# A dynamic convolution and two matmuls on one core: the tile of products in two parts, the softmax one superblock earlier, a slice of the products on VectorE, and other loads of x

## The chip, the cores and the metric

The kernel runs on one core of one Trainium2 chip. The metric is the device time of one execution in microseconds (us), the median over runs. Each core has TensorE (PE, with its weight loads shown apart as PEld), VectorE (DVE), ScalarE (ACT), GpSimd (POOL) and SyncE (SP), which here only issues transfers. The core's 16 DMA engines carry the transfers that SP issues (the profile calls that queue hardware_dynamic, q1) and those that POOL issues (software_dynamic, q0).

## The reference

The input x has 8 batches of 4096 tokens of 192 channels. For every token, each of 8 heads (24 channels each) has 7 weights; a softmax over the 7 weights mixes the token and the six tokens before it. The result goes through two matrices with an activation between them:

```python
w = exp(weight_gen - max);  w = w / sum(w)             # over the 7 taps
x_pad = concatenate([zeros(6 tokens), x])              # per batch: a batch starts with six tokens of zeros
y[s, h, g] = sum over k of w[s, h, k] * x_pad[s + k, h, g]
h = y @ w_in                                           # 192 -> 2048
out = (h - tanh(h)) @ w_out                            # 2048 -> 192
```

## The kernel before

**Tiling.** The 32,768 tokens are cut into NTOT = 32 superblocks of 1024 tokens, four to a batch (NSB = 4). Partition p of the 128 holds tokens 8p to 8p+7 of the superblock (J = 8), and six tokens of halo ahead of them, so a tile of x (`x_t`) is 128 rows of 14 x 192 float32, 10,752 bytes a row.

**The steps of one superblock n.**
- `load_wg` and `load_x` fetch the raw weights and x, through SP. In `load_x` the transfer `rows(0, P)` brings all 128 rows; at the first superblock of a batch (s == 0) a second one, `no_halo`, then writes zeros over the halo of row 0. It writes what the first wrote, so SP waits for the first to land. Superblock 0 has its own code: 112 rows and 15 rows for the halo.
- `softmax_exp` (ACT), `softmax_sum` in two halves (DVE), and `softmax_norm` (DVE: reciprocals into a spare corner of a PSUM tile, then `scale`) make the weights `wsm`.
- `products` (POOL) multiplies x with the seven taps into `pr`, a bfloat16 tile of 7 x 8 x 192 per partition, in a pool of two. In one instruction a tap has 1536 elements per partition. From superblock 5 on the order on POOL is: taps 0 and 1; the second sum of the superblock before (below); taps 2 to 5; `dma_sum`; tap 6.
- `dma_sum` is a transfer from POOL's queue that adds one part of `pr` to another inside SBUF: taps 3 to 5 onto 0 to 2. It leaves four parts (6, 0, 1, 2). For superblocks in `TWO_SUMS` (from 13 on, those whose number is no multiple of three), `second_sum` later adds tap parts 2 and 6 onto 0 and 1, and two parts are left. The second sum is issued from inside the next superblock's `products`, and POOL waits there until the first has landed. For superblocks 2 to 4 (`PART`) one sum leaves five parts.
- `conv_sums` (PE) adds the remaining parts and transposes them into PSUM (`pc`) by matmuls with an identity; with four parts there are 96 such matmuls in a superblock, with two 48. `conv_out` (ACT) copies them to `convT`.
- `gemm1` (PE) makes one of 16 blocks of the hidden layer in PSUM (`ph`, a pool of three that `pc` shares); ACT takes its tanh, DVE subtracts (`gt`).
- `out_stream` is the second matmul, as a stream of steps (16 to each of 8 token blocks) that `out_pairs` draws from; `store_out` copies a block out (ACT) and, once per superblock, SP stores it.

**The order.** The program is written in the order of the main loop, and each engine and SP's queue keeps that order. Pass n of the loop runs, for f = 0 to 15, `gemm1(n, f)` and the steps that `STEADY` puts behind that f: `pairs[f]` steps of the second matmul, which belong to superblock n-1; the transposes of superblock n+1 at f = 13 and 14 (`t2`, `t1`); the softmax of n+3 (exp at f = 1, sums at f = 2 and 5, scale at f = 14); and at f = 1 `products(n + 2)`. `load_x(n + 3)` stands at f = 7 (`X_AT`) and is tied behind that pass's last subtraction; `load_wg(n + 4)` at f = 1.

Of the kernel before, what the change touches and what calls it, by code (L numbers as in the profile page):

```python
# [8 lines left out]
FP32 = mybir.dt.float32  # L9
BF16 = mybir.dt.bfloat16  # L10
# [6 lines left out]
def kernel(  # L17
# [8 lines left out]
    nc = tc.nc  # L26

    B, S, D = x.shape
    H, K = weight_gen.shape[2], weight_gen.shape[3]
    G = D // H  # L30
# [10 lines left out]
    NTOT = B * NSB  # L41
    NFT = F // P
    NC = D // R
    PLAIN = (0, 1)
    PART = tuple(range(2,5))
    TWO_SUMS = tuple([n for n in range(13,NTOT) if n%3])
    SUM_FIRST = tuple(range(5,32))
    SCALE_TWICE = True
    assert S % TOK == 0 and D % R == 0 and F % P == 0
    assert NFT == 2 * J, "one token block of the second matmul per pair of f tiles"  # L50

    const = ctx.enter_context(tc.tile_pool(name="const", bufs=1))
    xpool = ctx.enter_context(tc.tile_pool(name="xpool", bufs=2))
    wgpool = ctx.enter_context(tc.tile_pool(name="wgpool", bufs=2))
    ppool = ctx.enter_context(tc.tile_pool(name="ppool", bufs=2))
    cpool = ctx.enter_context(tc.tile_pool(name="cpool", bufs=2))
    tpool = ctx.enter_context(tc.tile_pool(name="tpool", bufs=3))
    gpool = ctx.enter_context(tc.tile_pool(name="gpool", bufs=2))
# [25 lines left out]
    last_exp = {}  # L84
    last_conv = {}
    first_halo = {}

    def order(inst, other, reason):
        tc.add_manual_dep(
# [16 lines left out]
    def load_x(n, behind=None):  # L106
        b, s = divmod(n, NSB)
        s0 = s * TOK

        x_t = xpool.tile([P, HALO + J, D], FP32, name="x_t")  # L110

        def rows(p0, p1, r0=0, r1=HALO + J):
            first = x[0, 0:1]
            return nc.sync.dma_start(
                out=x_t[p0:p1, r0:r1, :],
                in_=bass.AP(
                    tensor=first.tensor,
                    offset=first.offset + (b * S + s0 + p0 * J - HALO + r0) * D,
                    ap=[[J * D, p1 - p0], [D, r1 - r0], [1, D]],
                ),  # L120
            )

        def no_halo():
            nc.sync.dma_start(
                out=x_t[0:1, 0:HALO, :],
                in_=zero[:].rearrange("o (h d) -> o h d", h=1).to_broadcast([1, HALO, D]),
            )


        if n == 0:  # L130
            rows(0, P, HALO, HALO + J)
            rows(16, P, 0, HALO)
            rows(1, 16, 0, HALO)
            no_halo()
        else:
            dma = rows(0, P)
            if behind is not None:
                order(dma, behind, "order of the loads")
            if s == 0:

                no_halo()
        x_of[n] = x_t

    def softmax_exp(n):
        wg_t = wg_of.pop(n)
        e_t = wgpool.tile([P, J, H, K], FP32, name="e_t")
        last_exp[0] = nc.scalar.activation(  # L147
            out=e_t[:].rearrange("p j h k -> p (j h k)"),
            in_=wg_t[:].rearrange("p j h k -> p (j h k)"),
            func=ACT.Exp,  # L150
        )
        e_of[n] = e_t

    def softmax_tile():
        return wgpool.tile([P, J, H, K], FP32, name="wsm")

    def softmax_sum(n, j0=0, j1=J):

# [10 lines left out]
            zr_of[n] = wgpool.tile([P, J * H], FP32, name="zr")  # L169
        nc.vector.reciprocal(zr_of[n][:, j0 * H : j1 * H], zsum_of[n][:, j0 * H : j1 * H])  # L170

    def softmax_norm(n, bank):

        wsm = softmax_tile()
        zr_v = bank[:, 512 - J * H : 512]
        nc.vector.reciprocal(zr_v, zsum_of[n][:])  # L176

        def finish():
            scale(nc.vector, wsm[:], e_of[n], zr_v)
            wsm_of[n] = (wsm, None, None, None)  # L180

        return finish

    def softmax_norm_ramp(n, bank):
# [25 lines left out]
            zr.rearrange("p (n o) -> p n o", o=1).to_broadcast([P, J * H, K]),  # L210
        )

    def dma_sum(pr, k0, k1, src0, src1, step=1):
        nc.gpsimd.dma_start(  # L214
            out=pr[:, k0:k1].rearrange("p k j d -> p k (j d)"),
            in_=pr[:, src0:src1:step].rearrange("p k j d -> p k (j d)"),
            accum_op=mybir.AluOpType.add,
            max_dma_last_dim=2 * J * D,
        )

    def products(n, taps=None, sums=None, hooks={}):

        x_t = x_of.pop(n)
        wsm, wsm_v, e_t, zr = wsm_of.pop(n)
        if e_t is not None:
            scale(nc.gpsimd, wsm[:], e_t, zr[:])

        pr = ppool.tile([P, K, J, D], BF16, name="pr")
        x_v = x_t[:]
        step = x_v.ap[0]  # L230

        def mul(eng, k0, k1, j0=0, j1=J):

            w = wsm_v if eng is nc.vector else wsm[:]
            nj = j1 - j0
            return eng.tensor_mul(  # L236
                pr[:, k0:k1, j0:j1, :].rearrange("p k j (h g) -> p k (j h) g", h=H),
                bass.AP(
                    tensor=x_v.tensor,
                    offset=x_v.offset + (k0 + j0) * D,  # L240
                    ap=[step, [D, k1 - k0], [G, nj * H], [1, G]],
                ),
                w[:, j0:j1]
                .rearrange("p j h (k o) -> p k (j h) o", o=1)[:, k0:k1]
                .to_broadcast([P, k1 - k0, nj * H, G]),
            )

        def parts(*ks):
            return [[pr[:, k] for k in ks]] * NC

        if taps is not None:
            for eng, k0, k1, j0, j1 in taps:
                m = mul(eng, k0, k1, j0, j1)
                if j1 == 1:
                    first_halo[0] = m
                if k0 in hooks:
                    hooks[k0]()
            prods_of[n] = parts(*sums)
            return

        if n in PLAIN:
            mul(nc.gpsimd, 0, 3)
            mul(nc.gpsimd, 3, 5)
            mul(nc.gpsimd, 5, K)
            prods_of[n] = parts(*range(K))
        elif n in PART:
            mul(nc.gpsimd, 0, 2)
            mul(nc.gpsimd, 2, 4)
            dma_sum(pr, 0, 2, 2, 4)
            mul(nc.gpsimd, 4, K)  # L270
            prods_of[n] = parts(4, 5, 6, 0, 1)
        else:
            mul(nc.gpsimd, 0, 2)
            second_sum(n - 1)
            mul(nc.gpsimd, 2, 6)
            if n in SUM_FIRST:
                dma_sum(pr, 0, 3, 3, 6)
            mul(nc.gpsimd, 6, K)
            if n not in SUM_FIRST:
                dma_sum(pr, 0, 3, 3, 6)  # L280
            if n in TWO_SUMS:
                to_sum[n] = pr
                prods_of[n] = parts(0, 1)
            else:
                prods_of[n] = parts(6, 0, 1, 2)
            if n == NTOT - 1:
                second_sum(n)

    def second_sum(n):

        if n in to_sum:
            dma_sum(to_sum.pop(n), 0, 2, 2, K, 4)

    def conv_sums(n, parts, pcs, home=None):

# [53 lines left out]
    def gemm1(n, f):  # L349
# [17 lines left out]
        last_act[0] = nc.scalar.activation(out=th[:], in_=ph_f, func=ACT.Tanh)  # L367
        last_sub[0] = nc.vector.tensor_sub(gt[:], ph_f, th[:])  # L368
        g_of.setdefault(n, []).append(gt)

    LAST = (NTOT - 1) * J
    half = {}
# [139 lines left out]
    for c in range(NC):  # L512
# [2 lines left out]
    nc.sync.dma_start(out=w_in[R:P, :, FA:F], in_=w_in[0:R, :, FA:F])  # L515
    products(
        1,
        taps=[(V, 0, 1, 0, J), (V, 1, 2, 0, J), (G_, 2, 5, 0, J), (G_, 5, 7, 0, J)],
        sums=range(K),
        hooks={2: load_w_out},  # L520
    )
    conv(0, (0, 1), (2,))
    softmax_exp(2)
    load_x(2)
    softmax_norm_ramp(2, obank[0])
    products(2)

    def some(sums, m):
        for _ in range(m):
# [24 lines left out]

    STEADY = dict(pairs=(4, 12, 0, 16, 0, 16, 0, 16, 0, 6, 10, 6, 10, 8, 8, 16), t1=(14, 8), t2=(13, 0), scale=14, sums=(2, 5))
    FIRST = dict(pairs=(4, 12, 0, 16, 1, 15, 0, 16, 0, 16, 0, 13, 3, 0, 16, 16), t1=(15, 2), t2=(11, 10), scale=15, sums=(1, 2, 3, 4, 8, 10))
    X_AT = 7

    def transposes(n, chunks):
        pcs = []
# [2 lines left out]
        conv_out(n, (chunks,), pcs)  # L565
        return pcs[0]

    for n in range(1, NTOT):
        more = n < NTOT - 1
        finish = None  # L570
        plan = FIRST if n == 1 else STEADY
        for f in range(NFT):
            gemm1(n, f)
            if n == 1:
                if f == 1:
                    load_wg(5)
# [5 lines left out]
                        step(m, h * JH, (h + 1) * JH)  # L582
                if f == 5:
                    wsm_of[3] = (softmax_tile(), None, e_of[3], zr_of[3])
                    products(3)
            elif f == 1:
                if n + 3 < NTOT:
                    softmax_exp(n + 3)
                if n + 4 < NTOT:
                    load_wg(n + 4)  # L590
                if n < NTOT - 2:
                    products(n + 2)
            if n > 1 and n + 3 < NTOT:
                for h, at in enumerate(plan["sums"]):
                    if f == at:
                        softmax_sum(n + 3, h * JH, (h + 1) * JH)
            if f == X_AT and n + 3 < NTOT:
                load_x(n + 3, last_sub[0])
            done = 0
            for chunks, at in sorted((((0, 1), plan["t2"]), ((2,), plan["t1"])), key=lambda c: c[1]):  # L600
                if more and at[0] == f:
                    out_pairs(at[1] - done)
                    done = at[1]
                    pc = transposes(n + 1, chunks)
                    if chunks == (2,) and n + 3 < NTOT:
                        finish = softmax_norm(n + 3, pc[:, 0])
            if finish is not None and f >= plan["scale"]:
                finish()
                finish = None
            out_pairs(plan["pairs"][f] - done)  # L610

    gemm2_last(0, 0, J)
# [34 lines left out]
```

The softmax here doesn't subtract the row's maximum and nothing guards it: scores larger than these inputs give would overflow.

## Time and profile before

| | |
|---|---|
| median of 3 runs | 754.72 us (754.22 to 755.33) |
| the profiled execution | 753.12 us, of it 751.4 us span |
| PE busy | 725.4 us, 97% |
| DVE busy | 664.6 us, 88% |
| POOL busy | 668.9 us, 89% |
| ACT busy | 638.8 us, 85% |
| DMA engines: POOL's queue, SP's queue | 35.7% and 27.6% of 16 engines' span |

Shares are of the span. A PE that is busy is not thereby at its peak, since its matmuls overlap. A row of the groups gives the line, engine and operation, what it writes and reads, its shape and how often it ran, then the time it was busy, the mean of one, and the idle time just before it with what ended that. A line of the waits gives who waited for whom: us in total, how often, the longest. In a timeline the first number is the start, the second the duration, "x3" three instructions merged. A line of the windows gives for a stretch of the span its length, then the busy time of each engine.

### The profile page before, as it was taken

Reading aid. Unit: us, or ns where it says so; the run is one execution under the profiler, and the core shown is the slowest. Engines: PE = TensorE matmul, PEld = TensorE weight load, DVE = VectorE, ACT = ScalarE, POOL = GpSimd, SP = SyncE. Lnnn points to the kernel's source line nnn. Section 1 sums busy time; section 2 is a strip of 40 time slices with the busy share of each in tenths; the row PEclk is TensorE's granted clock in tenths of the full one; section 3 lists DMA queues with packets and bytes.
Section 4 is the critical chain, followed back from the end, with each engine's and each line's share of the span. In section 5 each row is a group of like instructions: output and inputs, shape, how many; then the busy total and the mean of one; then the engine's idle time right before and its main releaser. Section 6 shows DMA issues by size and latency. Waiting matters only on the chain.

```text
span 751.4 us, 30497 instructions
## 1 busy us (share of the span) xinstructions
PE 725.4 (97%) x13928; PEld 567.6 (76%) x13928; DVE 664.6 (88%) x655; ACT 638.8 (85%) x872; POOL 668.9 (89%) x150
## 2 busy tenths in 40 slices
PE   3899999999999999999999999999999699999998
PEld 2477887787887777777777777777787577777777
DVE  7999889998889998999999999999989589998983
ACT  4888888888888888898989899898989588988883
POOL 7999999999999999999999999999999988999000
PEclk9999999999999999999999999999999899999999
DMA  8944526665655567785796777579668658673412
GB/s 234 242 111 107 171 109 173 187 181 126 191 149 170 169 170 160 202 196 163 196 229 151 180 203 185 169 196 215 173 157 192 180 139 189 183 177 85 113 44 86
DMA packets 32511, 124.99 MB, mean 166 GB/s; under 512 B 4495, under 2 KB 9343, under 8 KB 28414
## 3 DMA queue, kind: packets, MB, share of 16 engines
q0 software_dynamic: 17664, 46.01, 35.7%
q1 hardware_dynamic: 14718, 77.03, 27.6%
q8 instruction: 109, 1.79, 0.9%
q14 instruction: 20, 0.16, 0.1%
HBM read 54.52 MB, written 25.17 MB: 106 GB/s over the span
## 4 chain that ended last, share of the span: by engine, by line
PE 49%; DMA 4%; POOL 4%; issue 0%; ACT 0%; DVE 0%; POOLq 0%; DVEq 0%
PE obank L389 23%; PE ph L354 22%; DMA pr<-pr 4%; POOL pr L236 4%; PE pc L311 2%; PE po L432 1%; ACT th L367 0%; DVE wsm L207 0%; POOL pr L214 0%; ACT convT L337 0%; DVE pc L176 0%; DVE out_sb L446 0%; ACT ot L445 0%; DVE gt L368 0%; POOLq L214 0%
## 5 line engine op out<-in xcount | busy, mean ns | idle before, releaser
L368 DVE TENSOR_TENSOR gt<-ph,th 128x1024 bf16<-128x1024 f32 x512 | 603.1, 1218 | 66.8 <-ACT th L367 66.2
L236 POOL TENSOR_TENSOR pr<-x_t,wsm 128x3072 bf16<-128x3072 f32 (+3 forms) x95 | 629.7, 6816 | 8.1 <-PE obank L389 3.4
L367 ACT ACTIVATE th<-ph 128x1024 f32<-128x1024 f32 x512 | 506.8, 1026 | 71.1 <-PE ph L354 66.9
L354 PE MATMUL ph<-convT,w_in 64*128 64x512 bf16 x3072 | 407.3, 380 | 5.0 <-DVE gt L368 3.2
L389 PEld LDWEIGHTS <-gt 64*128 64x128 bf16 x7936 | 353.0, 94 | 73.0 <-issue 11.7
L389 PE MATMUL obank<-w_out,gt 64*128 64x192 bf16 x7936 | 399.5, 243 | 0.6 <-issue 0.5
L354 PEld LDWEIGHTS <-w_in 64*128 64x128 bf16 x3072 | 171.5, 95 | 82.7 <-issue 12.2
L408 ACT ACTIVATE out_sb<-obank 128x192 f32<-128x192 f32 x248 | 82.4, 332 | 12.9 <-PE obank L389 10.4
L214 POOL DMA_DIRECT2D pr<-pr x43 | 54.9, 1276 | 20.4 <-DMA pr<-pr 11.0
L311 PEld LDWEIGHTS <-pr 64*128 64x128 bf16 x2664 | 51.9, 102 | 24.1 <-POOL pr L236 10.2
L311 PE MATMUL pc<-ident,pr 64*128 64x64 bf16 x2496 | 50.7, 194 | 16.6 <-POOL pr L236 10.1
L337 ACT ACTIVATE convT<-pc 128x1024 bf16<-128x1024 f32 (+1 forms) x62 | 50.5, 816 | 7.3 <-PE pc L311 6.7
L161 DVE TENSOR_REDUCE zsum<-e_t 128x32 f32<-128x224 f32 (+1 forms) x61 | 23.6, 387 | 3.0 <-ACT e_t L147 3.0
L147 ACT ACTIVATE e_t<-wg_t 128x448 f32<-128x448 f32 x32 | 18.2, 569 | 7.3 <-DMA wg_t<-in_weight_gen_dram 7.3
L207 DVE TENSOR_TENSOR wsm<-e_t,pc 128x448 f32<-128x448 f32 x28 | 17.4, 621 | 3.3 <-POOL pr L236 0.5
L176 DVE RECIPROCAL pc<-zsum 128x64 f32<-128x64 f32 x28 | 15.4, 551 | 0.1
L432 PE MATMUL po<-w_out,gt 64*128 64x192 bf16 x256 | 11.2, 243 | 0.0
L236 DVE TENSOR_TENSOR pr<-x_t,obank 128x1536 bf16<-128x1536 f32 (+4 forms) x8 | 10.3, 1349 | 0.6 <-ACT wsm L199 0.6
L432 PEld LDWEIGHTS <-gt 64*128 64x128 bf16 x256 | 10.8, 93 | 0.0
L446 DVE TENSOR_TENSOR out_sb<-po,ot 128x192 f32<-128x192 f32 x8 | 2.9, 358 | 9.0 <-ACT ot L445 9.0
L445 ACT ACTIVATE ot<-po 128x192 f32<-128x192 f32 x8 | 2.6, 331 | 7.3 <-PE po L432 7.3
L467 POOL DMA_DIRECT2D w_in<-in_moe_w_in_dram x4 | 2.5, 628 | 3.0 <-ACT e_t L147 3.0
(19 smaller groups left out, 18.3 us busy)
## 6 DMA issues: line engine op xcount, KB each, us to landing
x_t<-in_x_dram SPq DMA_DIRECT2D x31, 1344.0 KB, 6.0
pr<-pr POOLq DMA_DIRECT2D x27, 1152.0 KB, 9.9
out_dram<-out_sb SPq DMA_DIRECT2D x31, 768.0 KB, 3.4
pr<-pr POOLq DMA_DIRECT2D x16, 768.0 KB, 6.8
wg_t<-in_weight_gen_dram SPq DMA_DIRECT2D x32, 224.0 KB, 6.8
x_t<-in_x_dram SPq DMA_DIRECT2D x1, 768.0 KB
w_out<-in_moe_w_out_dram POOLq DMA_DIRECT2D x1, 768.0 KB, 9.6
out_dram<-out_sb SPq DMA_DIRECT2D x4, 192.0 KB, 3.9
```

The costliest lines, as they stand in the source:

```text
L147: last_exp[0] = nc.scalar.activation(out=e_t[:].rearrange("p j h k -> p (j h k)"), in_=wg_t[:].rearrange("p j h k -> p (j h k)"), func=ACT ...
L161: nc.vector.reduce_sum(out=zsum_of[n][:, j0 * H : j1 * H], in_=e_of[n][:, j0:j1].rearrange("p j h k -> p (j h) k"), axis=AX.X,)
L214: nc.gpsimd.dma_start(out=pr[:, k0:k1].rearrange("p k j d -> p k (j d)"), in_=pr[:, src0:src1:step].rearrange("p k j d -> p k (j d)"), acc ...
L236: return eng.tensor_mul(pr[:, k0:k1, j0:j1, :].rearrange("p k j (h g) -> p k (j h) g", h=H), bass.AP(tensor=x_v.tensor, offset=x_v.offset ...
L311: nc.tensor.matmul(pc[r][:, col : col + R] if home else pc[:, r, col : col + R], lhsT=prods[c][gi][r * R : (r + 1) * R, 2 * j : 2 * j + 2] ...
L337: last_conv[0] = nc.scalar.activation(out=out, in_=pc[:, :, 0:cols].rearrange("p r (cj t) -> p r cj t", t=R), func=ACT.Copy,)
L354: nc.tensor.matmul(ph[:, r, :], lhsT=w_in[r * R : (r + 1) * R, c, f * P : (f + 1) * P], rhs=convT[r * R : (r + 1) * R, c, :], start=(c == ...
L367: last_act[0] = nc.scalar.activation(out=th[:], in_=ph_f, func=ACT.Tanh)
L368: last_sub[0] = nc.vector.tensor_sub(gt[:], ph_f, th[:])
L389: mm = nc.tensor.matmul(po[:, 0:D], lhsT=g_of[n][f][r * R : (r + 1) * R, col : col + P], rhs=w_out[r * R : (r + 1) * R, f, :], start=(r == ...
L408: last_act[0] = nc.scalar.activation(out=out_sb[:, j, :], in_=po[:, 0:D], func=ACT.Copy)
L432: nc.tensor.matmul(po[:, r, 0:D], lhsT=g_of[n][f][r * R : (r + 1) * R, col : col + P], rhs=w_out[r * R : (r + 1) * R, f, :], start=(f == 0 ...
```

## The change

1. `pr` becomes two tiles: `pa` with taps 0 to 3 (three buffers) and `pb` with taps 4 to 6 (one buffer). For superblock 1, taps 4 to 6 lie in two tiles borrowed from the pool of the output tiles.
2. POOL's order per superblock becomes: taps 0 and 1; taps 2 and 3; the second sum of the superblock before; taps 4 to 6; the first sum (`pa` 0 to 2 += `pb`).
3. From superblock 4 on (`HELP`), VectorE makes the last of the eight token columns of taps 0 and 1, 384 of the 10,752 elements. It stands at f = 3 of the pass and first copies the 16 weights into the `ph` tile that f = 3 has just left; POOL's first instruction leaves this column out.
4. `TWO_SUMS` holds every superblock from 13 to 31, also 15, 18, 21, 24, 27 and 30.
5. The softmax runs for n+4 instead of n+3. Pass 4 does two, and pass 5 does its own late. The exponential is written over the raw weights (`wg_t`, three buffers), and `wsm` has a pool of four. Its sums stand at f = 1 and 13.
6. `load_x(n + 3)` stands at f = 1 and is tied behind POOL's first instruction in `products(n + 2)`. At the first superblock of a batch (4, 8, ..., 28) the zeros go first, then one transfer brings row 0 without its halo, and one brings rows 1 to 127.
7. `pairs` is laid out differently; its sum is the same 128.

```diff
-    TWO_SUMS = tuple([n for n in range(13,NTOT) if n%3])
+    KA, KH = 4, 2
+    TWO_SUMS = (13, 14, ..., 31)
+    AHEAD = 4
+    HELP = (4, 5, ..., 31)
+    HELP_AT = 3
-    wgpool = ctx.enter_context(tc.tile_pool(name="wgpool", bufs=2))
-    ppool = ctx.enter_context(tc.tile_pool(name="ppool", bufs=2))
+    wgpool = ctx.enter_context(tc.tile_pool(name="wgpool", bufs=3))
+    papool = ctx.enter_context(tc.tile_pool(name="papool", bufs=3))
+    pbpool = ctx.enter_context(tc.tile_pool(name="pbpool", bufs=1))
+    wspool = ctx.enter_context(tc.tile_pool(name="wspool", bufs=4))
...
         else:
-            dma = rows(0, P)
+            if s == 0:
+                no_halo()
+                rows(0, 1, HALO)
+            dma = rows(1 if s == 0 else 0, P)
             if behind is not None:
                 order(dma, behind, "order of the loads")
-            if s == 0:
-                no_halo()
...
+        x_after[n + 1] = mul(nc.gpsimd, 0, KH, 0, J - 1 if n in HELP else J)
+        mul(nc.gpsimd, KH, KA)
+        second_sum(n - 1)
+        def rest(ph=None):
+            if n in HELP:
+                w = ph[:, 0, 0 : KH * H].rearrange("p (k h) -> p k h", k=KH)
+                nc.vector.tensor_copy(w, wsm[:, J - 1].rearrange("p h k -> p k h")[:, 0:KH])
+                nc.vector.tensor_mul(
+                    pa[:, 0:KH, J - 1, :].rearrange("p k (h g) -> p k h g", h=H), ...)
+            if n in PART:
+                dma_sum(pa[:, 0:2], pa[:, 2:4])
+            mul(nc.gpsimd, KA, K)
+            if n in PART:
+                prods_of[n] = parts(4, 5, 6, 0, 1)
             else:
-                prods_of[n] = parts(6, 0, 1, 2)
+                dma_sum(pa[:, 0:3], pb[:, 0:3])
+                if n in TWO_SUMS:
+                    to_sum[n] = pa
+                    prods_of[n] = parts(0, 1)
+                else:
+                    prods_of[n] = parts(3, 0, 1, 2)
+                if n == NTOT - 1:
+                    second_sum(n)
+        return rest
...
-    STEADY = dict(pairs=(4, 12, 0, 16, 0, 16, 0, 16, 0, 6, 10, 6, 10, 8, 8, 16), ..., sums=(2, 5))
+    STEADY = dict(pairs=(5, 11, 0, 16, 4, 12, 6, 10, 0, 6, 10, 8, 8, 8, 8, 16), ..., sums=(1, 13))
...
+        soft = [m for m in (n + 3,) * (n <= AHEAD) + (n + 4,) * (n >= AHEAD) if m < NTOT]
...
-            if f == X_AT and n + 3 < NTOT:
-                load_x(n + 3, last_sub[0])
+            if f == (9 if n == 1 else HELP_AT) and n + 2 < NTOT:
+                rest(ph)
+            if f == (9 if n == 1 else 1):
+                emit_x(n + 3)          # load_x(m, x_after.pop(m, None))
+                if soft and n != AHEAD and soft[0] + 1 < NTOT and n > 1:
+                    load_wg(soft[0] + 1)
```

## The prediction, made before the changed kernel ran

> **What bounds the kernel now.** I read the page's busy shares first, then the windows pass by pass, then the waits, POOL's timeline and the transfers.
>
> ```profile
> span 751.4 us, 30497 instructions
> ...
> PE 725.4 (97%) x13928; PEld 567.6 (76%) x13928; DVE 664.6 (88%) x655; ACT 638.8 (85%) x872; POOL 668.9 (89%) x150
> ```
>
> Four engines are nearly full. The windows tell which one sets the pace; each line is one pass, from its first subtraction to that of the next.
>
> ```profile
> 356.16:377.89 21.73, 21.73 (x406) 16.84 (x402) 20.29 (x21) 19.60 (x28) 21.37 (x6) 1.00 0.76 194
> 399.61:422.01 22.40, 22.40 (x454) 17.57 (x450) 20.36 (x21) 19.83 (x28) 22.10 (x6) 1.00 0.67 173
> 575.74:606.33 30.59, 24.62 (x406) 18.87 (x402) 20.54 (x22) 20.14 (x28) 26.68 (x7) 0.89 0.84 183
> ```
>
> After the length come PE, PEld, DVE, ACT and POOL. In a regular pass PE is busy all the time: 21.73 us with two parts to transpose, 22.40 with four. DVE has 1.4 us to spare. The third line is pass 25, the one real stop; the waits of that stretch name it:
>
> ```profile
> PE pc L311 <- DMA pr<-pr: 6.0, 1, 6.0
> ```
>
> PE waited for a second sum that POOL had issued late. POOL's timeline over one superblock shows how close it runs:
>
> ```profile
> 376.96 6.09 POOL L236 TENSOR_TENSOR pr<-x_t,wsm 128x3072 bf16<-128x3072 f32 x1
> 383.00 1.25 POOL L214 DMA_DIRECT2D pr<-pr  x1
> 383.77 11.57 POOL L236 TENSOR_TENSOR pr<-x_t,wsm 128x6144 bf16<-128x6144 f32 x1
> 395.64 1.28 POOL L214 DMA_DIRECT2D pr<-pr  x1 [0.30 <-POOL pr L236]
> 396.46 19.99 POOL L236 TENSOR_TENSOR pr<-x_t,wsm 128x1536 bf16<-128x1536 f32 x3
> ```
>
> Tap 6 (2.86 us, then the next product starts at 399.32) closes it: 22.36 us a superblock, above PE's 21.73. So the kernel is PE-bound, with POOL right behind.
>
> The view of the transfers (per queue the packets, MB and share of 16 engines; per kind how often, KB each, us to landing), and last the same view of the window 232 to 238 us, which holds one load of x alone:
>
> ```profile
> q0 software_dynamic: 17664, 46.01, 35.7%
> q1 hardware_dynamic: 14718, 77.03, 27.6%
> ...
> x_t<-in_x_dram SPq DMA_DIRECT2D x31, 1344.0 KB, 6.0
> pr<-pr POOLq DMA_DIRECT2D x27, 1152.0 KB, 9.9
> ...
> pr<-pr POOLq DMA_DIRECT2D x16, 768.0 KB, 6.8
> ...
> x_t<-zero SPq DMA_DIRECT2D x8, 4.5 KB
> x_t<-in_x_dram SPq DMA_DIRECT2D x1, 67.5 KB
> ```
> ```profile
> q1 hardware_dynamic: 144, 1.38, 63.5%
> ```
>
> **The change part by part.**
>
> *Two sums from 13 on, and the new pace of POOL.* Passes 12 to 30 would all take 21.73 us: 412.9. They now take 427.3 (289.0 to 716.3). The gain of 14.4 is six passes at 0.67, 8.85 from pass 25, 1.3 from pass 12 and 0.3 from pass 23. It needs a POOL that keeps up. A product costs 1.82 ns an element (5.59 us from start to start for 3072). The new superblock is 4.9 (2688 elements) + 6.07 (3072, to the end) + 0.78 (issue of the second sum) + 9.09 (4608, 8.79 and the 0.30 ahead of an issue) + 0.82 = 21.65, just under PE's 21.73; with one sum 20.4, which lets POOL run ahead in passes 4 to 11. The first sum now has 0.82 + 4.9 + 6.07 = 11.8 us to land before POOL wants it, where it had 9.3 and takes 9.9.
>
> *The slice on VectorE.* A product of 384 elements took 547 ns, one of 192 353 ns; that is 1.01 ns an element and 159 fixed, so the copy of 16 is some 0.17. With the 0.10 seen between dependent steps, less 0.08 of overlap, 0.74 us a pass: DVE 21.0 of 21.73. I take nothing for it, since PE's new `pairs` leave work between the blocks after f = 3. Bounds: 0 and 0.3 us in 28 passes, 8 us.
>
> *Softmax one ahead, exp in place, other order of `pairs` and sums.* The same instructions, one pass earlier; pass 4 does two softmaxes, 1.9 us of DVE against 2.2 idle there. With the ramp of the single `pb` I take +1.5, bounds 0 and 4.
>
> *The loads of x.* This decides. At superblocks 4, 8, ..., 28 one transfer now brings 127 rows, where it brought 128. How many engines share it? The packets of SP's queue tell. Rows moved: x 31 x 128 + 128 + 112 + 15, stores 35 x 128, weights 32 x 128, the copy of `w_in` 192, zeros 8 x 6: 13,039. The queue had 14,718, and the 1,679 left over are 101 x 16 + 15 + 8 x 6: one closing packet for each engine that took part. So 101 transfers ran on 16 engines, that of 15 rows on 15 and each zero fill of six rows on 6. In every one the rows split into equal shares. 127 is a prime: the ends are 16 engines with unequal shares (6.0 us, as now) and one engine. The nearest row is that of 15 rows, the only other odd count, and it too split evenly, so I take one engine.
>
> What does one engine need? In the window, 63.5% of 16 engines over 6.0 us is 61.0 us for 128 rows, 0.476 each. In the packet records the shortest and the median row take 0.404; the longer ones lie at a load's start, where sixteen begin at once. So 127 rows take 51.3 us (taken: one engine has no such crowd) to 60.5.
>
> [...]
>
> That engine also carries its share of the sums: 24 packets of 283 ns (6.8 us) of a first, 16 of 276 (4.4) of a second. Do they wait for the load or go between its rows? A second sum issued at 585.56, 0.4 us before a load, moved nothing until that load's rows were through and took 11.3 us instead of 6.8; a load issued 2.7 us behind a sum moved its first row after 3.8 us instead of 1.0. So 8 or 16 packets in a row are not broken up; of 127 no row tells. I take them as let in: in every collision the engines changed hands after 8 or 16, and 127 without a turn would be new. The other end is kept.
>
> [...]
>
> Now the path. The load of x for 4m is tied behind POOL's first product of superblock 4m-1, 4.9 us into it. From there: 1.0 to the first packet, 1.8 for the tail of the running sum, 51.3, 4.4 + 6.8 for the sums issued meanwhile, 0.4 to landing: 65.7 us (61.3 without a second sum). POOL has 16.8 of work left in that time, then stands still. So does DVE, whose slice waits at f = 3 of pass 4m-2 for the same x, with all later subtractions behind it, and PE runs out of `ph`. SP's next weights and store lie behind those rows in the same queue, and ACT's exp waits for them, inside the same stop. A batch is 3 x 21.65 + 4.9 + 65.7 = 135.6, against 86.9 for PE.
>
> Landings: superblock 4: POOL's first product of 3 ends at 58.9 as now, + 1.0 + 51.3 + 4.4 + 0.4 = 116.0. Superblock 8: + 70.9 (19.9; 25.7 with 5.3 of waiting until the transposes of 4 have left the single `pb`; 20.4; 4.9) + 61.3 = 248.2. 12: + 66.1 + 61.3 = 375.6. 16: + 67.4 + 65.7 = 508.6. 20, 24, 28: + 135.6 each = 915.3. Then 85.8 to the last first sum, 9.5 to its landing, 6.6 for the second, and 41.7 from the last transposes to the end, as now (709.7 to 751.4): 1059. Around the span lie 1.7, and the median stands 1.6 above the profiled execution: **1062 us**.
>
> **The rivals.**
>
> 1. *The 127 rows go over 16 engines.* Then every load takes 6 us: 751.4 - 14.4 + 1.5 + 3.3 = **742**, faster (738 to 752 by the bounds). For it: the bytes per row are unchanged, and the 14.4 us are read off the windows. Against it: the closing packets. It decides if a load lands within 16.8 us of its tie.
> 2. *One engine, but the sums wait behind the load.* Its window is 52.7: 111.6; 235.2; 354.0; 474.1; then 122.6 each, 841.7; + 143.6 + 3.3 = **989**.
> 3. *One engine at 0.476 a row*: + 9.2 in each of seven loads, **1126**.
> 4. *Sixteen engines, and x hits the first sum*: the load now starts 5.7 us behind a first sum and adds up to its 3.8 us of engine time; the sum lands after 13.3 instead of 11.8, POOL waits 1.5 in 19 superblocks, less the some 6.5 us that it runs ahead by superblock 13 (2 us gained a pass): + 22, **764**. Against it: sums that a store meets in the same way land after 9 to 11.5 now. Slower from 1.0 us a superblock on.
>
> **How the numbers follow.** Main case 0.62 (own range 1035 to 1090), rival 2 0.14, rival 3 0.12, rival 1 0.10, rival 4 0.02. The range takes the three one-engine cases with their ends, 970 to 1130: 0.88, less a twelfth for what lies outside, 0.81. Slower 0.89, faster 0.10, within 0.2% (1.5 us, what a measurement of this kernel can tell) 0.01.
>
> **What would show it.** Right: x of 127 rows landing 50 to 70 us after its issue; POOL's first product of superblocks 4, 8, ..., 28 waiting some 45 us for x; DVE and PE with seven gaps; PE's share of the span near 70%; passes between the gaps near POOL's 21.65. The transfer's closing packets would be one. Wrong: these loads landing after 6 to 10 us; then the windows from pass 12 on should read 21.73 and pass 25 should have lost its stop. DVE's two new instructions should take 0.55 and about 0.17 in either case.

## The result and the profile after

The changed kernel takes **1074.91 us** (1073.45 to 1079.89) against 754.47 us (752.67 to 755.33) for the kernel before in the same comparison: a ratio of 1.426 with a 95% interval of 1.421 to 1.432, slower by 320 us. The forecast was 1062 us, range 970 to 1130. The profiled execution has a span of 1071.7 us. Ratios here and below are taken over the undisturbed runs alone, so they need not be the quotient of the medians.

The page of the changed kernel, first the busy shares, then two rows of the span in 40 slices:

```profile
span 1071.7 us, 30071 instructions
...
PE 747.6 (70%) x13640; PEld 573.1 (53%) x13640; DVE 687.4 (64%) x711; ACT 642.0 (60%) x872; POOL 656.5 (61%) x157
...
PE   5860599804999069980599805997159972599998
...
DMA  8620435422674137841488414794147851378621
```

PE has fallen from 97% to 70%. The seven holes in PE's row come with low values in the row of the DMA engines: the machine stands still while the transfers are nearly idle too. The waits of the changed kernel say for what (who waited for whom: us in total, how often, the longest):

```profile
POOL pa L252 <- DMA x_t<-in_x_dram: 286.6, 6, 49.4
...
ACT wg_t L151 <- DMA wg_t<-in_weight_gen_dram: 225.8, 8, 45.6
...
DVE pa L286 <- DMA x_t<-in_x_dram: 47.4, 1, 47.4
```

POOL waited six times nearly 50 us for x; a seventh stop, of 42.8 us, the view puts down to "issue". VectorE's slice waits for x as well, and ACT for the weights that lie behind x in SP's queue. POOL's timeline around one stop:

```profile
466.14 1.28 POOL L218 DMA_DIRECT2D pa<-pb  x1 [0.30 <-POOL pb L252]
515.89 4.93 POOL L252 TENSOR_TENSOR pa<-x_t,wsm 128x2688 bf16<-128x2688 f32 x1 [48.46 <-DMA x_t<-in_x_dram]
```

The load of this x was issued at 450.74, and its last row was through 64.4 us later. The seven loads of 127 rows took 57.7 to 65.4 us from issue to last row, where a load of 128 rows in the same kernel took 5.5 to 8.9. The transfers of the changed kernel, per queue and for the two new kinds of load (how often, KB each):

```profile
q0 software_dynamic: 19296, 50.73, 27.1%
q1 hardware_dynamic: 14620, 76.99, 21.4%
...
x_t<-in_x_dram SPq DMA_DIRECT2D x7, 1333.5 KB
...
x_t<-in_x_dram SPq DMA_DIRECT2D x7, 6.0 KB
```

As many rows are moved as before, 13,039. So 14,620 - 13,039 = 1,581 are closing packets (the packet records of this queue hold 1,581 of 4 bytes): 94 x 16 + 15 + 8 x 6 are accounted for by the other transfers, and 14 are left for the seven loads of 127 rows and the seven of one row. That is one for each, so each ran on one engine. The records of the rows agree: in the seven long loads they follow one another, no two at once for more than 0.04 us.

Between the stops the passes look as forecast, with two exceptions (the windows of the changed kernel; each line is one pass: length, then PE, PEld, DVE, ACT, POOL):

```profile
543.75:565.61 21.86, 21.86 (x406) 16.63 (x402) 21.04 (x22) 19.70 (x27) 21.31 (x6) 1.00 0.85 201
616.25:677.79 61.54, 23.42 (x406) 17.95 (x402) 21.33 (x22) 19.95 (x27) 25.31 (x6) 0.72 0.34 94
858.35:888.48 30.13, 24.69 (x406) 18.77 (x402) 21.27 (x24) 20.18 (x27) 15.52 (x4) 0.89 0.48 98
```

The first is an undisturbed pass, 21.86 instead of 21.73. The second, pass 18, holds a stop. The third, pass 25, comes before a stop: the transposes wait for a second sum that the long load held up.

### The profile page after: what moved, and what is told of

Read it like the earlier page. It is cut to its first block, busy times and chain, and to the rows that moved or that the text cites. A ratio compares the mean times of both kernels' runs of the same rounds, so it can differ in the third digit from the quotient of the medians.

```text
span 1071.7 us, 30071 instructions
## 1 busy us (share of the span) xinstructions
PE 747.6 (70%) x13640; PEld 573.1 (53%) x13640; DVE 687.4 (64%) x711; ACT 642.0 (60%) x872; POOL 656.5 (61%) x157
## 3 DMA queue, kind: packets, MB, share of 16 engines
q1 hardware_dynamic: 14620, 76.99, 21.4%
## 4 chain that ended last, share of the span: by engine, by line
POOL 31%; another core or an unknown queue 30%; PE 21%; issue 11%; DMA 4%; DVE 2%; ACT 1%; SPq 0%; POOLq 0%; DVEq 0%; ACTq 0%
POOL pa L252 18%; PE obank L414 10%; PE ph L378 9%; POOL pb L252 9%; POOL pa L218 4%; DMA pa<-pa 2%; DMA w_out<-in_moe_w_out_dram 1%; PE pc L335 1%; PE po L457 1%; DVE gt L392 1%; DMA wg_t<-in_weight_gen_dram 0%; ACT th L391 0%; DVE pa L252 0%; SPq L119 0%
## 5 line engine op out<-in xcount | busy, mean ns | idle before, releaser
L414 PE MATMUL obank<-w_out,gt 64*128 64x192 bf16 x7936 | 422.1, 248 | 222.4 <-ACT out_sb L433 217.9
L252 POOL TENSOR_TENSOR pa<-x_t,wsm 128x3072 bf16<-128x3072 f32 (+2 forms) x63 | 338.3, 5548 | 330.0 <-DMA x_t<-in_x_dram 286.6
L378 PE MATMUL ph<-convT,w_in 64*128 64x512 bf16 x3072 | 426.7, 386 | 51.9 <-DVE pa L286 47.2
L252 POOL TENSOR_TENSOR pb<-x_t,wsm 128x4608 bf16<-128x4608 f32 (+2 forms) x33 | 281.1, 8518 | 11.0 <-PE pc L335 10.9
L165 DVE TENSOR_REDUCE zsum<-wg_t 128x32 f32<-128x224 f32 (+1 forms) x61 | 23.7, 389 | 218.2 <-ACT wg_t L151 218.2
L151 ACT ACTIVATE wg_t<-wg_t 128x448 f32<-128x448 f32 x32 | 18.3, 571 | 225.8 <-DMA wg_t<-in_weight_gen_dram 225.8
L433 ACT ACTIVATE out_sb<-obank 128x192 f32<-128x192 f32 x248 | 81.3, 328 | 18.5 <-PE obank L414 18.2
L335 PE MATMUL pc<-ident,pa 64*128 64x64 bf16 x1920 | 43.2, 197 | 35.0 <-DMA pa<-pa 33.5
L335 PEld LDWEIGHTS <-pa 64*128 64x128 bf16 x2016 | 42.3, 104 | 44.3 <-issue 37.8
L218 POOL DMA_DIRECT2D pa<-pb x27 | 34.7, 1284 | 8.5 <-POOL pb L252 7.4
L218 POOL DMA_DIRECT2D pa<-pa x22 | 33.7, 1533 | 9.2 <-DMA pa<-pb 8.3
L335 PE MATMUL pc<-ident,pb 64*128 64x64 bf16 x288 | 6.5, 202 | 10.5 <-POOL pb L252 8.9
L335 PEld LDWEIGHTS <-pb 64*128 64x128 bf16 x360 | 7.5, 105 | 11.2 <-POOL pb L252 8.9
L457 PE MATMUL po<-w_out,gt 64*128 64x192 bf16 x256 | 11.2, 243 | 0.0
```

Of the source, the lines that this page charges most:

```text
L151: last_exp[0] = nc.scalar.activation(out=wg_t[:].rearrange("p j h k -> p (j h k)"), in_=wg_t[:].rearrange("p j h k -> p (j h k)"), func=AC ...
L165: nc.vector.reduce_sum(out=zsum_of[n][:, j0 * H : j1 * H], in_=e_of[n][:, j0:j1].rearrange("p j h k -> p (j h) k"), axis=AX.X,)
L218: return nc.gpsimd.dma_start(out=out.rearrange("p k j d -> p k (j d)"), in_=in_.rearrange("p k j d -> p k (j d)"), accum_op=mybir.AluOpTyp ...
L252: return eng.tensor_mul(prod(k0, k1)[:, :, j0:j1].rearrange("p k j (h g) -> p k (j h) g", h=H), bass.AP(tensor=x_v.tensor, offset=x_v.offs ...
L335: nc.tensor.matmul(pc[r][:, col : col + R] if home else pc[:, r, col : col + R], lhsT=prods[c][gi][r * R : (r + 1) * R, 2 * j : 2 * j + 2] ...
L378: nc.tensor.matmul(ph[:, r, :], lhsT=w_in[r * R : (r + 1) * R, c, f * P : (f + 1) * P], rhs=convT[r * R : (r + 1) * R, c, :], start=(c == ...
```

## The experiments

### One suspect at a time: the load of x

Four kernels were compared with the kernel before (753.29 us there). The first is the changed kernel with the 127 rows split into 15 and 112:

```diff
-            dma = rows(1 if s == 0 else 0, P)
+            parts = [rows(1, 16), rows(16, P)] if s == 0 else [rows(0, P)]
             if behind is not None:
-                order(dma, behind, "order of the loads")
+                for dma in parts:
+                    order(dma, behind, "order of the loads")
```

> The changed kernel with one edit: at superblocks 4, 8, ..., 28 the 127 rows come as two transfers of 15 and 112 rows, which have 15 and 16 equal shares. Theory (a transfer runs on the largest number of engines up to 16 that divides its rows, so 127 rows run on one): the load lands 6 to 9 us after its issue, POOL never waits some 48 us for x, the seven stops are gone, and the time is 742 to 750 us: the undisturbed passes of the changed kernel, 22.44 and 21.86 us, in place of the long ones give a span near 745. Rival (the stops come from the tie of the load behind POOL's product, from the single pb or from the slice on VectorE): the stops remain, above 1000 us.

Measured: 757.6 us (756.68 to 758.51), ratio 1.0057 (1.0037 to 1.0077). All seven stops are gone, and 317 of the 320 us with them. Its queue of SP shows the engines (with the same 13,039 rows, 14,830 leaves 1,791 = 94 x 16 + 15 + 8 x 6 + 7 x (16 + 15 + 1)):

```profile
q1 hardware_dynamic: 14830, 77.00, 29.6%
```

The cause holds, the level was missed: it was to be faster than before and is 0.6% slower. That is taken up below.

The second run does the reverse, in the kernel before: zeros first, then row 0, then 127 rows, and nothing else.

```diff
-            dma = rows(0, P)
+            if s == 0:
+                no_halo()
+                rows(0, 1, HALO)
+            dma = rows(1 if s == 0 else 0, P)
...
-            if s == 0:
-                no_halo()
```

> The kernel before with one edit: its loads of x at superblocks 4, 8, ..., 28 become the zeros, row 0 and one transfer of 127 rows. Theory: the load alone makes the loss. It lands some 60 us after its issue at f = 7 of a pass, where POOL wants it after some 11, and each batch of four passes takes 130 to 136 us instead of 89: 1040 to 1110 us, POOL waiting for x seven times. Rival (the load is slow only together with the new tie, pools and slice): about 755 us.

Measured, in one run: 1076.87 us. Its waits:

```profile
POOL pr L236 <- DMA x_t<-in_x_dram: 332.2, 8, 51.3
...
PE pc L311 <- DMA pr<-pr: 173.2, 13, 50.6
```

The load alone is enough for a loss of this size: 1076.87 us here, 1074.91 with the whole change. What the other parts add or save can't be read beside it.

The third tells a rule about shares from "an odd number is bad": the changed kernel with 5 and 122 rows, 122 being even but dividing only by 2 below 16.

```diff
-            dma = rows(1 if s == 0 else 0, P)
+            parts = [rows(1, 6), rows(6, P)] if s == 0 else [rows(0, P)]
```

> The changed kernel with the 127 rows cut into 5 and 122. 122 is 2 x 61. Theory of the largest divisor: two engines, 61 rows each, 24.6 us by 0.404 a row and some 39 us to landing with the sums let in; POOL stops for some 22 us seven times; 880 to 910 us. The queue's closing packets: two for each 122 rows, five for each 5 rows. Rival (a count that does not fill 16 engines evenly falls to one engine): stops of some 45 us, 1030 to 1070 us.

Measured, in one run: 893.87 us, span 892.1. Waits and queue:

```profile
POOL pa L253 <- DMA x_t<-in_x_dram: 132.2, 6, 23.1
```
```profile
q1 hardware_dynamic: 14662, 76.99, 25.9%
```

14,662 - 13,039 = 1,623 = 94 x 16 + 15 + 8 x 6 + 7 x (2 + 5 + 1): two engines for 122 rows, five for five. POOL's longest wait fell from 49.4 to 23.1.

The fourth asks whether POOL can do with a second sum in every superblock from 13 on without the rest of the change:

```diff
-    TWO_SUMS = tuple([n for n in range(13,NTOT) if n%3])
+    TWO_SUMS = tuple(range(13,NTOT))
```

> The kernel before with one edit: the second sum at every superblock from 13 on. Theory: PE would save 0.67 us in six passes, 4.0 us, but POOL's superblock with a second sum takes 22.36 us and more where it waits for the first sum to land, against 21.73 for PE, so the stop seen in pass 25 comes more often: 756 to 770 us, slower. Rival (PE alone sets the pace and the stop in pass 25 was a chance collision): 746 to 751 us.

Measured: 768.18 us (765.97 to 770.53), ratio 1.0207 (1.017 to 1.0244). Undisturbed passes read 21.73, as the forecast read them off the windows, but passes 18, 22 and 27 take 31.47, 27.76 and 30.49. The waits name the second sum, once in each of them:

```profile
PE pc L311 <- DMA pr<-pr: 17.7, 3, 7.4
```

So POOL with 22.36 us a superblock falls behind PE with 21.73. In each of the three passes the second sum was issued within 1.2 us of a load of x and landed after 10.5 to 11.6 us, where the others took 6.5 to 8.5. What spares the mended kernel these stops is told by two runs below. With its loads of x back at f = 7 its passes 12 to 30 take 440.2 us, as much as here (440.4); without the slice they take 420.1, with it 418.4. So it is mainly the earlier load of x with its new tie, which keeps the load 4.6 to 5.1 us ahead of the second sum however late POOL is (place and tie were not tried apart); the slice is worth under 2 us there.

### Why the mended kernel is not faster than before

The kernel with 15 + 112 rows has a span of 756.7, where rival 1 counted 738.5 (751.4 - 14.4 + 1.5). Pass by pass the difference of 18.2 lies in two places. Passes 12 to 30 take 418.4 instead of 412.9: the undisturbed ones 21.86, and eight of 22.0 to 22.4. Passes 2 to 11 take 239.5, which is 13.8 more than before, where 1.5 was allowed; nearly all of it is in passes 3 (28.16 against 22.75), 4, 5, 8, 9 and 10. Two of them in the windows of that kernel:

```profile
206.78:231.98 25.20, 22.66 (x455) 17.71 (x451) 21.09 (x22) 19.88 (x27) 24.90 (x6) 1.00 0.78 190
231.98:256.39 24.41, 22.66 (x454) 18.34 (x451) 21.18 (x23) 20.09 (x27) 24.11 (x5) 1.00 0.67 175
```

PE's timeline in the first of these passes (start, us; in brackets the idle time before and its end):

```profile
225.98 1.15 PE L415 MATMUL obank<-w_out,gt 64*128 64x192 bf16 x23
229.67 0.57 PE L415 MATMUL obank<-w_out,gt 64*128 64x192 bf16 x9 [2.54 <-issue]
```

PE stood still in the middle of a stream of like matmuls and waited for nothing that the profile shows. The packets of the queue that the profile calls "instruction" give a hint. They have 16,384 bytes:

| PE idle in passes 3 to 10 from (us) | for | a packet of instructions ended | PE went on, us behind it |
|---|---|---|---|
| 88.57 | 0.98 | 89.18 | 0.4 |
| 106.42 | 2.08 | 107.38 | 1.1 |
| 135.05 | 0.90 | 134.51 | 1.4 |
| 156.56 | 0.83 | 155.97 | 1.4 |
| 227.13 | 2.54 | 228.03 | 1.6 |
| 250.14 | 1.75 | 250.52 | 1.4 |
| 276.74 | 1.46 | 276.76 | 1.4 |

There are 106 such packets in the span, one in 7 us, so a packet that ended 1.1 to 1.6 us ahead of PE's restart in six of seven cases is hardly chance. (In the first case the view names ACT's copy of an output block as what PE waited for, in the other six nothing.) PE seems to have run out of instructions; that is argued, since the profile does not say for which engine a packet is. The transfers of that kernel in the window 227 to 228.2, which holds one such packet:

```profile
q0 software_dynamic: 60, 0.18, 106.9%
q8 instruction: 1, 0.02, 5.1%
```

A first sum kept the engines full around it. That the packet was late because of such transfers is argued from this, not shown: the six packets took 0.89 to 1.37 us, with 0.98 as the median of all 106, so none was slow once it had begun. The idle times are 10.5 of the some 14 us. In pass 3 the granted clock adds to them: behind the idle time of 2.08 us it stood at 0.5 for 3.4 us. The kernel before has, between 64 and 690 us and beside the stop of pass 25, one idle time of PE over 0.4 us: 0.64 at 291.18.

Four kernels, all with 15 + 112 rows, looked for the cause, beside the kernel before at 752.63 us (746.98 to 756.35). The first takes the old layout of `pairs`:

```diff
-    STEADY = dict(pairs=(5, 11, 0, 16, 4, 12, 6, 10, 0, 6, 10, 8, 8, 8, 8, 16), ...)
+    STEADY = dict(pairs=(4, 12, 0, 16, 0, 16, 0, 16, 0, 6, 10, 6, 10, 8, 8, 16), ...)
```

> The changed kernel with its rows cut into 15 and 112 (the run of 757.6 us), and the old pairs (4, 12, 0, 16, 0, 16, ...). There an undisturbed pass with two parts takes 21.86 us, with four 22.44, against 21.73 and 22.40 in the kernel before. Theory: the longer passes come from the new layout, which changes once more between the two matmuls (at f = 4 and 5); with the old one they read 21.73 and the time falls by some 3 us, 753 to 756. Rival (the slice on VectorE makes them longer, and the old layout leaves PE nothing between f = 2 and 3 and f = 4 and 5 to cover it): passes of 21.9 to 22.2, 757 to 764 us.

Measured: 762.59 us (759.24 to 766.99), ratio 1.0133 (1.0101 to 1.0166): worse, the rival was right. Two of its passes, 24 with the slice and 30, in which there is nothing left to slice:

```profile
569.87:592.00 22.13, 21.91 (x406) 16.73 (x402) 20.89 (x24) 19.71 (x28) 21.13 (x6) 1.00 0.84 191
703.44:725.17 21.73, 21.73 (x406) 16.84 (x402) 18.85 (x17) 19.29 (x27) 0.00 (x0) 1.00 0.10 39
```

With the old layout the slice costs PE 0.39 us a pass. The new layout alone costs 0.08 (pass 30 of the kernel with it: 21.81) and brings the slice's price down to 0.05 (21.86, against 21.81 in the run without the slice below).

The second puts the loads of x back to f = 7, behind the last subtraction; the third does that and takes the old `pairs` too:

```diff
+            if f == 7 and n + 3 < NTOT:
+                load_x(n + 3, last_sub[0])
...
-                emit_x(n + 3)
```

> The changed kernel with its rows cut into 15 and 112, and the loads of x back at f = 7 behind that pass's last subtraction, while the weights stay at f = 1. Theory: passes 3 to 10 lose some 14 us because x, the first sum, a store and the weights now meet within a few us, and the transfers that fetch PE's instructions wait behind them (PE's idle times there each end when such a fetch of 16 KB runs); with x at its old time most of that goes: 743 to 749 us. Rival (the loss comes from the single pb and from the two softmaxes of pass 4): 755 to 759 us.

> Both edits, the old pairs and the loads of x at f = 7, on the changed kernel with its rows cut into 15 and 112. If both theories hold, the gains add: 740 to 746 us, faster than the kernel before by more than 1%. If the slice needs the new pairs, no better than the run with x at f = 7 alone.

Measured: 777.06 us (769.09 to 781.62), ratio 1.0303 (1.026 to 1.0346), and 777.26 (770.1 to 788.02), 1.0276 (1.0231 to 1.0321). Both missed by 30 us. In the second kernel the slow passes 5 and 8 to 10 stayed (24.2 to 25.3), so the new place of the loads is not their cause, and this theory fell. Passes 3 and 4 read 22.85 and 23.45 there, where 28.16 and 23.71 stood; whether the place of the loads did that stays open, since pass 3 also fell, to 23.42, when the slice alone was taken away (below). Instead new waits came, in the second kernel:

```profile
POOL pa L253 <- DMA x_t<-in_x_dram: 22.0, 10, 5.4
...
PE pc L336 <- DMA pa<-pa: 16.3, 6, 7.5
```

POOL now comes for x before it has landed, and the second sums meet the loads again, with stops in passes 18 (31.81) and 26 (30.66), where a second sum was issued within 0.7 us of a load. Loading x early, behind POOL's first product, is a part of the change that pays.

The fourth takes the slice away:

```diff
-    HELP = (4, 5, ..., 31)
+    HELP = ()
```

> The changed kernel with its rows cut into 15 and 112, and no slice on VectorE: POOL makes all of taps 0 and 1. Theory: the slice costs PE nothing, its passes stay at 21.86 us where nothing stops them, DVE's idle time in them rises from 0.8 to 1.5 us, and POOL needs 22.4 us a superblock from 13 on; it falls behind by some 0.5 us a pass and uses up its lead, and stops come late in the span: 757 to 766 us. Rival (the slice itself holds PE): undisturbed passes below 21.8 us and a time of 750 to 756.

Measured: 756.57 us (750.44 to 758.19), ratio 1.0029 (0.9995 to 1.0062): no difference from the kernel before can be told, and the time lies between the two ranges. The single times lie in two groups, four at 750.4 to 750.8 and six at 755.4 to 758.2, and the profile belongs to the first. In it, passes 8 to 10 are clean:

```profile
203.73:226.13 22.40, 22.40 (x454) 17.57 (x450) 20.54 (x21) 19.85 (x27) 22.10 (x5) 1.00 0.72 173
226.13:248.53 22.40, 22.40 (x454) 17.58 (x450) 20.54 (x20) 19.85 (x27) 22.10 (x6) 1.00 0.74 172
```

Passes 3 to 5 are not (23.42, 24.90, 24.20), and from 13 on POOL falls short without the slice: eight passes take 22.1 to 23.0, and the transposes wait for what POOL did late. The waits between 300 and 650 us:

```profile
PEld L336 <- POOL pb L253: 6.5, 6, 1.6
```

The last try in this line is therefore the slice from superblock 13 on only:

```diff
-    HELP = (4, 5, ..., 31)
+    HELP = (13, 14, ..., 31)
```

> The changed kernel with 15 + 112 rows, and VectorE's slice only from superblock 13 on, where POOL has two sums to issue. Theory: the slice is not needed before (POOL runs ahead there), and the idle times of passes 8 to 10 came with it, so passes 7 to 11 read 22.4 as without the slice (7 us less than with it), and passes 12 to 30 as with it (418): 749 to 752 us, faster than the kernel before by up to 0.6%. Rival: the late instruction fetches of passes 3 to 10 don't depend on the slice and come at other places: 755 to 758.

Measured: 753.24 us (752.06 to 760.76), ratio 1.0024 (0.9994 to 1.0054) against 753.74: no difference can be told, and the time lies between the two ranges. Passes 7 to 11 came as expected, 112.4 us in all where the slice made it 118.6. But passes 14 to 17 now read 22.51, 23.39, 22.87 and 22.41, with idle times of 0.4 to 1.2 us behind a packet of instructions in three of them. So the rival was right in this: such idle times move with every change of the program. What decides where they fall stays open.

### A version that beats both

The stop of pass 25 in the kernel before is the same mechanism as those of the kernel with every second sum: a second sum comes late because POOL is a little too slow. By its timeline three superblocks took it 66.6 us from 396.46 and 67.1 from 463.06, against 65.86 for three passes of PE. The trace shows how this lag becomes a stop. The ten second sums of superblocks 13 to 26 were issued 6.9, 5.6, 5.8, 5.2, 5.0, 4.8, 3.7, 3.4, 2.7 and 0.4 us ahead of the next load of x. The first nine landed after 6.5 to 7.6 us, the last after 11.3. PE's wait for it is 6.0 of the 8.85 us that the stop cost. The rest goes with the granted clock, the third number from the right in the windows of the kernel before:

```profile
595.90:602.70 6.80, 5.66 (x90) 4.69 (x92) 0.97 (x1) 2.70 (x4) 6.20 (x3) 0.50 0.54 111
```

It stood at 0.5 for these 6.8 us. Six matmuls of `gemm1`, which took 0.83 us just ahead of the stop, took 1.51 in it.

To be rid of the stop needs no new tiles. Leaving two second sums out gives POOL its time back:

```diff
-    TWO_SUMS = tuple([n for n in range(13,NTOT) if n%3])
+    TWO_SUMS = tuple([n for n in range(13,NTOT) if n%3 and n not in (22, 26)])
```

> The kernel before with one line changed: superblocks 22 and 26 too get no second sum. My theory of the level is that POOL's second sums decide where PE stops: POOL needs 22.36 us a superblock with one and gains about 1.3 us where one is left out. In the kernel before POOL drifted behind until the second sum of superblock 26 was issued at 585.56, 0.4 us before a load of x, and PE stopped in pass 25 for 8.85 us. By this theory the stop is gone: minus 8.85, plus 2 x 0.67 for 48 more transposes each, that is 745 to 748 us. The rival: the stop only moves to a later pass, 752 to 758.

Measured: **745.9 us** (745.37 to 746.54) against 753.74, ratio 0.9908 (0.9879 to 0.9937). The page's busy shares and pass 25 in the windows of this kernel:

```profile
PE 722.1 (97%) x14024; PEld 564.1 (76%) x14024; DVE 664.6 (89%) x655; ACT 638.6 (86%) x872; POOL 666.4 (90%) x148
```
```profile
576.60:599.00 22.40, 22.40 (x454) 17.57 (x450) 20.36 (x22) 19.82 (x28) 22.08 (x6) 1.00 0.67 173
```

96 matmuls more, and 7.8 us less; the slowest of its runs (746.54) is faster than the fastest of the kernel before (747.34). PE has no idle time of more than 0.4 us between pass 13 and the end of pass 30. With 20, 23 and 26 left out instead:

> The kernel before with three second sums fewer (20, 23 and 26). By the same theory no stop in any pass and three times 0.67 us more: 746 to 748 us. Slower than the run with two fewer by 0.7 us if neither has a stop, faster than it by several us if that one still has a stop behind pass 26. The rival, that the stop comes from the load of x alone and not from POOL's lag, gives 753 to 757.

Measured: 746.83 us (745.66 to 748.33), ratio 0.992 (0.989 to 0.995). No stop either. It is 0.9 behind the version with two fewer, where 0.7 was expected, though the two overlap. Both versions also leave out the second sum of superblock 26, the very one that met the load, and leaving out that one alone was not tried; so the times do not tell POOL's lag from this one meeting. The traces do: with superblock 22 left out, the second sum of 23 is issued 5.7 us ahead of the load instead of 3.4 and that of 25 5.3 instead of 2.7, and in both versions no second sum comes closer to a load than 4.7. The stop needed both, the lag and the load that it ran into.

## Why the prediction was right, point by point

**127 rows on one engine.** Right. This term is the whole result: split so that 15 and 16 engines share it, the loss is gone, and alone in the kernel before it makes one as large. The rows of the trace before could not decide it, since every count in them split evenly; one engine for 127 was the author's estimate from that, and the runs with 127, 122 and 112 rows show it. By their closing packets 127 rows took one engine, 122 two, 112 sixteen, 15 fifteen and 5 five. All five counts fit the theory that the run with 112 rows was to test; what holds for others, these runs don't tell.

**0.404 us a row.** Right: in the long loads the median row took 0.404 to 0.405 us, the mean 0.414 to 0.423 (all 127 rows 52.6 to 53.7 us instead of 51.3). Rival 3 with 0.476 is out; that figure came from a load's start: in the window 232 to 238 us of the kernel before the first 16 rows took 0.59 to 1.25 us each, most of the rest 0.404.

**The sums get in between the rows.** Right, and the part that decided between 989 and 1062. A first sum that met a long load landed after 21 to 22.4 us instead of 8.9 to 10.6, a second after 16.4 to 16.5 instead of 6.9 to 10.4. From their issue to the end of the load it was 46 to 60 us. But it did not go as in the two collisions of the kernel before, from which the forecast took it, where 8 or 16 packets went in a row. The transfers in the window 217.4 to 223.2 us, which lies inside one long load and one first sum:

```profile
q1 hardware_dynamic: 9, 0.10, 4.0%
q0 software_dynamic: 9, 0.03, 2.4%
```

Nine rows and nine packets of the sum, 6.4% of 16 engines, which is one engine without a pause. They take turns one by one: a row, then a packet of the sum, and the next row begins 0.65 us after the last. In the seven loads there are 16, twice 24 and four times 40 such places, as many as the sums had packets for that engine. So the turn came after every row, not after 8 or 16 packets as in the collisions; what makes the difference, no run here tells.

**The landings.** From issue to POOL's restart it took 58.2, 61.7, 61.2, 65.1, 66.0, 65.1 and 65.0 us; the forecast had 57.1, twice 61.3 and four times 65.7. That is closer than its terms: the rows took 1.3 to 2.4 us more than counted, and the sums' packets between them 3.7, 5.5 and 9.2 us instead of 4.4, 6.8 and 11.2. The two errors cancel in part, and that is luck. The batches from superblock 16 on took 136.3, 135.05 and 135.3 against 135.6.

**The 12.7 us that are missing** (a span of 1071.7 for 1059) lie in two steps of that sum. From the landing of superblock 4 to that of 8 it took 138.9 instead of 132.2: POOL waited twice for the transposes to leave the single `pb`, 5.0 and 5.9 us, where one wait of 5.3 was counted. And the tail behind the last stop took 149.2 instead of 143.6: it was made from POOL's pace, but by then PE was the later one (the last second sum had landed at 1024.4, the transposes began at 1029.24). The remaining 0.4 are spread over the other steps. The 3.3 us between span and median came as 3.2.

**The slice at nothing for PE, and 21.73 a pass.** Too low by 0.13 us a pass: with the new `pairs` 0.08 and the slice 0.05. The reason given (the new layout leaves work for PE) is right, since without that layout the slice costs 0.39, more than the upper bound of 0.3. DVE's two new instructions took 0.55 and 0.19 us as worked out (0.55 and 0.17).

**"+1.5 for the ramp and the single `pb`", bounds 0 and 4.** Wrong, though it didn't matter beside the stops. In the mended kernel passes 2 to 11 lost 13.8. The step that failed is the clause "the same instructions, one pass earlier": it has no term for times in which PE stands still behind a packet of instructions (9.6 us in six cases), nor for the half clock in pass 3. What makes them stays open. Rival 1, had it come, would have ended near 758 and not at 742.

**Two sums from 13 on.** Half right. Pass 25's stop and the six passes of 22.40 were there to be gained: passes 12 to 30 of the mended kernel are 8.9 us shorter than before, of 14.4 forecast. That is what the stop alone is worth (8.85), and by leaving second sums out most of it is to be had.

## What to carry to other kernels

Before a load is cut, count how many engines will share it: a change of one row in 128 moved the load from 16 engines to one and cost 46 us in each of seven places. A profile shows it in two numbers, the time from issue to landing and the queue's packets less the rows it moved. And where two engines run within 3% of each other, look first for the few steps where the slower one falls behind: two operations taken away there were worth more here than seven parts of rebuilding.

## What the runs showed of the hardware that was not expected

- PE stopped for 0.8 to 2.5 us in the middle of like matmuls, six times of seven 1.1 to 1.6 us behind the end of a 16 KB packet of instructions. It cost the mended kernel some 10 us of PE's time in passes 3 to 10, and where it happens changed with each version. No run here shows that PE lacked instructions, or what made a packet late.
- While one engine was busy with 127 rows for 57 to 63 us, first sums landed after 21 to 22.4 us instead of 8.9 to 10.6. In the window 217.4 to 223.2, inside such a load and such a sum, the two queues kept 6.4% of the 16 engines busy, which is that one engine.
- On that engine the two queues took turns after every row of 10,752 bytes: from the start of one row to that of the next it was 0.65 us, with one packet of a sum between them.
- Behind an idle time of PE of 6.0 us (kernel before, pass 25) the granted clock stood at 0.5 for 6.8 us, behind one of 2.1 us (mended kernel, pass 3) for 3.4 us; behind one of 2.5 us (mended kernel, pass 8) it stayed at 1.00.
